# Retention layer and token/channel mixer on one core: decay on v instead of k in two batches, v of the first pair loaded first, tables made one by one

## The chip, the core and the metric

The kernel runs on one core of a Trainium2 chip. The metric is the device time of one execution in microseconds (us); the time given is the median of several executions. The engines are named as the profile names them: PE (matrix products; PEld is its weight load), DVE (vector engine), ACT (scalar engine), POOL (which here issues nearly all loads) and SP (which issues the first load, the transposes made by DMA, and most stores).

## The reference

For batch b (4), head h (8), 768 tokens and 64 dimensions a head, with a decay per head:

```
gamma = 1 - 2 ** (-5 - h);  scale = 1 / 8
state = gamma * state + outer(k[t], v[t])          # per token t
y[t]  = scale * q[t] @ state
x = y with heads side by side: [4, 768, 512]
h = relu(x^T @ w_tok1) @ w_tok2;   u = x + h^T     # mixing over tokens, 768 -> 256 -> 768
out = u + relu(u @ w_ch1) @ w_ch2                  # mixing over channels, 512 -> 1536 -> 512
```

## The kernel before, in words

Two heads form a pair; a batch has four pairs. In the text k00 is the k of batch 0, pair 0, and so on. `front(b, p)` handles a pair in six chunks of 128 tokens:

- Three loads bring k, q and v of the pair from fp32 in memory to fp16 in the core (line 284, and line 278 for the q of batches 0 and 1). Only k00 is loaded as fp32, by SP, into a buffer named `us` (set `HARD`, line 141).
- `decayed` (lines 322 for ACT, 324 for DVE) multiplies k by a decay per token, one instruction for each of the two heads; the result goes to a buffer of tag `k16`, of which there are three.
- `turn` transposes k and q. In batches 0 and 1 PE does it: k with six products of 128 by 128 (line 348), q with twelve that write 64 rows each, a head at a time (line 346). k is copied out of the bank by DVE or ACT (line 361). q is multiplied on the way out by a table `gq` (line 356), made by ACT from an exponential, 384 wide for each pair (line 222). In later batches most turns go through DMA transposes on SP.
- Products of k and v give the states of the chunks (line 377, ten small products); DVE accumulates them with decay (lines 387, 389); ACT or DVE spreads them into `r` (lines 398, 401).
- Scores are products of the turned k and q (line 417), masked by DVE (line 427); masked scores times v (line 438) and `r` times q (line 447) give y in a bank.
- Then come the token mixer, products with `wt1` (line 467), a relu (lines 476, 478), products with `wt2` (line 487), copies to u and X (lines 493, 503), and the turn of u (line 533, copied out at line 540, or by DMA).

`back(b)` is the channel mixer. In batches 0 and 1 `widen` multiplies u with `wc1` (line 571; 96 products of 128x384 a batch), with a relu on ACT (line 587). In batches 2 and 3 `widen7` does it with seven products in the place of eight (line 644), with sums on DVE and a relu of two tiles at once on DVE (line 690). `narrow7` multiplies by `wc2` (lines 785 and 795), keeps partial results (line 775) and adds them into X (line 802), which is stored (line 832).

The order of all this work, on every engine, the choice of engine where there are two, and the bank of each result are in one table, `PLAN` (line 40), read by `placed` (line 72). A `+` in it is followed by a number of products of zeros on PE that nobody reads (line 906, called fillers here). The costs written at each operation are those with which such a table was planned; they don't act when the kernel runs. Each engine's queue is in order.

Of the kernel before, what the change touches and what calls it, by code (L numbers as in the profile page):

```python
# [21 lines left out]
class Op:  # L22
# [18 lines left out]
    "04050b000f010d0c0g03020e1h11i00907+e1n4061j51o1p1l10a2r01k11R01m+32v50i2w0h1q1r1s2s11S11u26+91v411x0j2t31T01w1"  # L41
    "U01V51z08+31A01W1y0l1X10k1Y2452260m1t01B1Z1D42u0+125651E31027+32x22820293203360n2y0p2z212A+23531C0340222B0q362"
    "C2F511F02a60r2302I2D0+22d32b2e0o2J2E251G12H1H2N51I02G2K22L3f712M02c11J1K01L01M2f12O3i3j1N12g73711O00s2P12h1P43"
    "8393a3H02i00z3b1Q03c2j0u2m2k03I2l03D12Q42n03n12R3e072S03E13h2p62T0t2W0x3F73d02U00y3g3k02q12o12V03l3o3G12X04f60"
    "v3m04g3p02Z33q43012Y03r0A3s14b03Q65273Rah33t3U3w4c0ae63S3T3u03z43x04d73B3A13J53C1af4e0agai4J13y03v13K4K13LaO4a"
    "R7aSaPaj3Man60E3NaQ3Y2ao4L0ak4aT3OaC53P10waDalapaEaU73V63WaV3Z4M1aW4P04h10B3X1400aI74iam0DaL54QaJ414424RaX34S0"
    "CaMaK4304T4U4j4kaYaZ441d451aF4aG47az7aN1baA460aw5191eaBat65h1axauaH4lbf4ay1fbg4mav5i00H1a1c4o10530I4804N6aq7ar"
    "4pbhbi4bjas4sb334904Obk4q5j14rb44W26045k14n0b07b654Y4t1b10Gb54V0bo504ub2bl6bp4Z4v0bmb74w34xbc7bn4z0151gbu64a4X"
    "4y0bvb84A164B0544b9555bd0F5Q0ba51252be4F4Cbs7bq1817bb5300Kbr4D0bKbt05704G0bO55604H00L4E05R0bxbwbLby158bz65n3bM"
    "5W15o5900PbP0bA0M5X5l0bB5a5T05p5YbT5U05ZbNbD5b06r05dbC0bU05m60bGbX5q5rbE61bH5V5e0ca65sc65f00S5Sc75u1043bY06s0c"  # L50
    "b1cc75yc2bV35vcd6o0c35x6p00JcfbQ55t05w5C05z4bWc8cg00O0N5A7u10R6t5D620bRbZc95B0c05c0cj5F7c15E0ck14I5G631523bS65"
    "645H0co5I5L5J06667ch55K1cp6870Q69ci6u26b45M06a06c5g5O36e16v6d16q6wclbF6f6x5N06y5P06g06zcT3cs6cmct6W1cU6kcu6B02"
    "51cV6E0Wc50cE66A1cF6D6X0d23d3cG6h7v0cN5cO6Fcv6cw7x10Td4db2cx6CcP6J16Z1cQ3bI0cR6G0cH5cScIdc6K6i16Hcecn6l16j0726"
    "c41dd7017A76Y6m0cy2cK3czcJ8A17y07Bd547CcL0V7D6I173cAd8571cr0dw2dxd60X7EcM7FcZ7d7dyd96L074cW3d00Yd17z6M2cX7w756"
    "N76da7G0dh4cB777cCdq6dr6O08B0781de5cYcDbJ0di820dk2dldjdf6Pdsdn7dCdt3dm0UdodpdudgdDdz4dA8318CdFdvdG2796735dEdBd"
    "H1dN46Q06n6S7c6T0dL6R17ddO7a6V7b6U0e23dM0dY850dRdP7e6dQ08D0dS7H01758E07fdU7g08617h47ie0847K0Ze97e307j07L7J7k11"
    "47P57Q7l7IeadVdTed877M07N7m113dZeee18827O08G17n8H7R0898F8a7q7o07r08b7S77T8c7p08I8J8de7dI67U08K7Y7s08LdJe80ek12"
    "el7Vem7W0eb8f41267Z0818i80011ec0eo77t8g7X0ep18jev58M0e44et8h8N0126e5enew8Re6egeh8Pez8k4ef8n68e0eu08QeA9b08l8oe"
    "x8m08Oeq38q18p08rey0eC9G08S0ercq18s09808T9H18teK39c0eG8u0eD8weY78V1eM5eL8x08WeBdKeHeZ8v08y0991eIeNeJes10eOf29M"
    "49e69I9Nf028U09f8Y58X08Zf1ePf3eR9gf5eQ2900eS9194f69O9h9ieW9PeT9j9Qfc9dff5eUf46920eXfgfa950fh3fj9k1fb9R9J1f7ft4"  # L60
    "fkfdf8fv79aej1960eVfu930fmfif9fwfnfl2fx9l0136frfyfA9K0fK7fBfLfo9ofsfpfHfz3fF9pfqg06fCfY5fZfO9n9mfDfPfIfM2g2fGg"
    "1fNg39q19r9s09t0fRfEfe9ug59v1g46eE1gcg6fSeF0fQ3g7fJ9w29L9xgafWfTg8fU9y09zgb9Cg9gj69S0fX8zfVgdh17gegB979A09D09B"
    "0gCgD9E0gF4gf9T51309XgggM29UgG09WgKgk0gogH5gL09VgNgp1gEa11a2gIgO9Y39ZgQh20a00gP1a30gTa45a5a60gJghhn0gRgXgsgUa7"
    "aagt09FgYh0a81ei0gq4gl2giab0gZgrgmac1h35gxguh4gSa90gyhjdW1h6h82hB5h70hogvgnh9hagwadhb0hChkhchlhp1hD3hdhrhFhqhm"
    "hshfhEhghuhGh5hvhIht6hH4hwhJhzhehNi61hxhOhPgW1hS7hyi7hi1ic5hAiahU6hThKhVi80ibhWhXidiD2i9iehLhZiiiB0ifhMi0ighQi"
    "ki4in4iCgA0hY3iFihip5ioiEi1iqiriH6hRiGi2iPijisi5iIiJiuit1iviW7hh0i3imiKiziwiLiX0iAiNilixji3gz1iQiOiMiyiRiSjE2i"
    "UiTiY6jejgjk5j1iZjj0j31j20jp4j5jlgV1iVj4j7jF0dX1j0jfjnj60jmjhjo0jajG5j8jqjtj9jbjrjAjs0jBjCjDjujvjd0jJjL1jMjc0j"
    "HjwjK0jxjNjIjO0jPjy1jz1jQjW1jRjSjV0jTjUjY0jX1"
# [27 lines left out]
def kernel(  # L96
# [44 lines left out]
    HARD = {(0, 0, "k")}  # L141
# [22 lines left out]
    def one(eng, cost, emit):  # L164
        return [(eng, cost[0], cost[1], emit)]
# [127 lines left out]
    def front(b, p):  # L293
# [22 lines left out]
        def decayed(tag, src, dep, g, hard):  # L316
            dst, got = Slot(tag), []
            for j in range(2):
# [7 lines left out]
                got.append(op(either(emit, ACT=(506, 610), DVE=(335, 420) if hard else (232, 312)),  # L326
# [3 lines left out]
        K, kl = decayed("k16", KF, kd, gk, (b, p, "k") in HARD)  # L330

        def turn(src, dst, dep, mode):
# [31 lines left out]
        if TURN[b, p, "q"] == "w":  # L364
            qt = turn(QF, QT, [qd], "w")
        else:
            Q, ql = decayed("q16", QF, qd, gy, False)
            qt = turn(Q, QT, ql, "x")
# [570 lines left out]
```

## Time and profile before

| what | value |
|---|---|
| time, median of three runs | 187.66 us (187.24 to 189.37) |
| the profiled execution's own time | 188.25 us |
| its span in the trace | 186.5 us |
| PE busy | 178.7 us, 96% |
| DVE busy | 164.9 us, 88% |
| ACT busy | 122.6 us, 66% |
| POOL busy | 53.4 us, 29% |

The profiled execution took 1.75 us more than its span, and 0.59 us more than the median. Engines work side by side; a wait costs time where nothing else fills it. A busy PE isn't PE at its peak: the rows count a product from its start to the end of its result, so products that overlap fill the row though they may not follow each other at the full rate. Where a text speaks of an instruction's row, its columns are start, length, engine, line, operation, result <- operands with shapes, count, and in brackets the idle time before it and what ended it.

### The profile page before, as it was taken

Reading aid. Unit: us, or ns where it says so; the run is one execution under the profiler, and the core shown is the slowest. Engines: PE = TensorE matmul, PEld = TensorE weight load, DVE = VectorE, ACT = ScalarE, POOL = GpSimd, SP = SyncE. Lnnn points to the kernel's source line nnn. Section 1 sums busy time; section 2 is a strip of 40 time slices with the busy share of each in tenths; the row PEclk is TensorE's granted clock in tenths of the full one; section 3 lists DMA queues with packets and bytes.
Section 4 is the critical chain, followed back from the end, with each engine's and each line's share of the span. In section 5 each row is a group of like instructions: output and inputs, shape, how many; then the busy total and the mean of one; then the engine's idle time right before and its main releaser. Section 6 shows DMA issues by size and latency. Waiting matters only on the chain.

```text
span 186.5 us, 5228 instructions
## 1 busy us (share of the span) xinstructions
PE 178.7 (96%) x2083; PEld 135.6 (73%) x2083; DVE 164.9 (88%) x433; ACT 122.6 (66%) x284; POOL 53.4 (29%) x65
## 2 busy tenths in 40 slices
PE   7987999999999999999999999999999999999991
PEld 3554788676678988866668988875688986667880
DVE  3798999868999998989259999999999999799992
ACT  3668588857879775677885586999793425773220
POOL 8996775455422008902000750000000000000000
PEclk9999999999999999999999999999999999999999
DMA  8999999999999979999993999880533040511045
GB/s 117 163 159 196 179 175 191 179 193 205 178 162 150 137 78 131 181 182 194 158 218 65 114 148 134 143 189 22 88 98 102 37 118 10 218 62 54 4 158 182
DMA packets 94377, 25.51 MB, mean 137 GB/s; under 512 B 84368, under 2 KB 91536, under 8 KB 94352
## 3 DMA queue, kind: packets, MB, share of 16 engines
q0 software_dynamic: 67456, 13.18, 90.6%
q1 hardware_dynamic: 25168, 9.11, 26.6%
q10 hardware_dynamic: 1728, 2.88, 4.5%
q8 instruction: 16, 0.26, 0.6%
q14 instruction: 9, 0.07, 0.1%
HBM read 26.74 MB, written 6.29 MB: 177 GB/s over the span
## 4 chain that ended last, share of the span: by engine, by line
PE 82%; DMA 7%; DVE 6%; POOL 1%; issue 1%; ACT 1%; DVEq 0%; POOLq 0%
PE bank L571 17%; PE bank L644 15%; PE bank L785 15%; PE bank L795 11%; DMA q<-in_q_dram 7%; PE bank L487 6%; PE bank L467 5%; PE bank L417 3%; DVE X L802 3%; PE bank L438 3%; PE bank L447 2%; PE bank L346 1%; PE bank L377 1%; PE bank L533 1%; DVE hs L749 1%; DVE qT L356 1%
## 5 line engine op out<-in xcount | busy, mean ns | idle before, releaser
L571 PE MATMUL bank<-uT,wc 128*128 128x384 f16 x192 | 35.6, 326 | 0.2 <-DVE uT L540 0.2
L427 DVE TENSOR_TENSOR am<-bank,mask 128x384 f16<-128x384 f32 x64 | 32.8, 548 | 1.0 <-PE bank L417 0.9
L284 POOL DMA_DIRECT2D v<-in_v_dram x16 | 16.7, 1043 | 42.8 <-PE bank L447 22.1
L587 ACT ACTIVATE h<-bank 128x384 f16<-128x384 f32 x48 | 22.0, 494 | 8.4 <-PE bank L571 8.0
L571 PEld LDWEIGHTS <-wc 128*128 128x128 f16 x192 | 17.4, 98 | 9.7 <-DVE uT L540 0.2
L785 PEld LDWEIGHTS <-hs 128*128 128x128 f16 x216 | 20.4, 98 | 3.5 <-DVE hs L749 0.5
L775 ACT COPY us<-bank 128x256 f32<-128x256 f32 x29 | 10.6, 378 | 18.8 <-PE bank L785 18.2
L661 DVE TENSOR_TENSOR h<-bank,us 128x384 f16<-128x384 f32 x36 | 18.7, 550 | 1.7 <-PE bank L644 0.9
L785 PE MATMUL bank<-wsum,hs 128*128 128x256 f16 x144 | 19.5, 273 | 0.0
L656 ACT COPY us<-bank 128x384 f32<-128x384 f32 x36 | 16.4, 489 | 4.6 <-PE bank L644 3.7
L802 DVE TENSOR_TENSOR X<-X,bank 128x256 f32<-128x256 f32 x48 | 19.0, 412 | 0.1
L389 DVE SCALAR_TENSOR_TENSOR U<-U,gs,bank 128x64 f32<-128x64 f32 x64 | 16.5, 277 | 1.1
L284 POOL DMA_DIRECT2D k<-in_k_dram x15 | 15.4, 1035 | 6.6 <-ACT u L493 2.4
L493 ACT CAST u<-bank 128x384 f16<-128x384 f32 x27 | 12.5, 483 | 5.6 <-PE bank L487 5.3
L453 ACT CAST x<-bank 128x384 f16<-128x384 f32 x25 | 11.6, 489 | 6.3 <-PE bank L447 6.3
L795 PEld LDWEIGHTS <-h 128*128 128x128 f16 x144 | 13.7, 98 | 1.8 <-DVE am L427 0.2
L644 PE MATMUL bank<-hs,wsum 128*128 128x384 f16 x72 | 14.8, 326 | 0.0
L467 PE MATMUL bank<-x,wt 128*128 128x128 f16 x192 | 14.5, 219 | 0.1
L749 DVE TENSOR_TENSOR hs<-h 128x768 f16<-128x768 f16 x20 | 10.9, 551 | 3.7 <-ACT h L587 3.7
L487 PE MATMUL bank<-h,wt 128*128 128x128 f16 x192 | 14.2, 219 | 0.0
L802 DVE TENSOR_TENSOR X<-X,us 128x256 f32<-128x256 f32 (+1 forms) x25 | 13.0, 534 | 0.6 <-ACT x L453 0.5
L487 PEld LDWEIGHTS <-wt 128*128 128x128 f16 x192 | 12.1, 98 | 1.5
(86 smaller groups left out, 361.2 us busy)
## 6 DMA issues: line engine op xcount, KB each, us to landing
v<-in_v_dram POOLq DMA_DIRECT2D x16, 192.0 KB, 9.2
q<-in_q_dram POOLq DMA_DIRECT2D x16, 192.0 KB, 8.6
out_dram<-X SPq DMA_DIRECT2D x12, 256.0 KB, 2.4
k<-in_k_dram POOLq DMA_DIRECT2D x15, 192.0 KB, 8.5
wc<-in_moe_w_ch_dram POOLq DMA_DIRECT2D x5, 512.0 KB, 13.4
out_dram<-X ACTq DMA_DIRECT2D x10, 256.0 KB, 2.4
wt<-in_moe_w_tok_dram POOLq DMA_DIRECT2D x2, 384.0 KB, 8.9
wc<-in_moe_w_ch_dram POOLq DMA_DIRECT2D x2, 256.0 KB, 10.1
```

The lines of the kernel that those rows point to most:

```text
L284: (nc.sync if hard else nc.gpsimd).dma_start(out=s.tile, in_=src.rearrange("h (c p) d -> p h c d", p=P))
L389: nc.vector.scalar_tensor_tensor(out=u[:, c], in0=u[:, c - 1], scalar=gs[:, p:p + 1], in1=st, op0=ALU.mult, op1=ALU.add)
L427: nc.vector.tensor_tensor(am, SC[g].tile[:, :m * P].rearrange("p (i t) -> p i t", t=P), mask.to_broadcast([P, m, P]), ALU.mult)
L467: nc.tensor.matmul(acc[:, jt * P:(jt + 1) * P], wt1[:, i, jt * P:(jt + 1) * P], X16.tile[:, i], start=(i + jt == 0), stop=(i == NC - 1), s ...
L487: nc.tensor.matmul(Y[hf].tile[:, i * P:(i + 1) * P], wt2[:, jt, t], H1.tile[:, jt], start=False, stop=(jt == NJ - 1), skip_group_check=True)
L571: nc.tensor.matmul(acc[:, :SH], wc1[:, ct, ft * P:(ft + 1) * P], UT.tile[:, ct, sh * SH:(sh + 1) * SH], start=(ct == 0), stop=(ct == NP - 1))
L587: nc.scalar.activation(H2.tile[:, ft], A.tile[:, :SH], AF.Relu)
L644: nc.tensor.matmul(acc[:, :SH], left(ct), r[:, ct], start=first and ct == 0, stop=ct == 1, skip_group_check=True)
L661: nc.vector.tensor_tensor(into(hf)[:, ft], bank.tile[:, :SH], kept(j), ALU.add)
L785: nc.tensor.matmul(acc_[:, lo], l[:, j], r[:, j], start=first and j == 0, stop=j == K2 - 1, skip_group_check=True)
L795: nc.tensor.matmul(acc_[:, lo], l[:, j], r[:, j], start=first and j == 0, stop=j == K2 - 1, skip_group_check=True)
L802: (nc.vector if e == "DVE" else nc.gpsimd).tensor_tensor(dst(), dst(), b_(), ALU.add)
```

## The change

In batches 0 and 1 (`ON_V`) the decay multiplies v instead of k, still in a buffer of tag `k16`; k goes to its turn and to the state products as it was loaded. The two forms are equal, since only the product of k and v, or of the scores and v, is used. As k is then laid out a head at a time, its turn on PE takes twelve products with 64 rows instead of six with 128. The first pair's v is the load that comes as fp32 through SP, and its k comes through POOL. The table `gq` becomes four operations, of which each pair waits for its own. The turn of u of batch 0's last pair uses two banks instead of one, and the relu over two tiles in `widen7` may go to ACT (six of eighteen do). `PLAN` is another table: fillers go from 37 to 30.

```diff
-    "04050b000f010d0c0g03020e1h11i00907+e1n4061j51o1p1l10a2r01k11R01m+32v50i2w0h1q1r1s2s11S11u26+91v411x0j2t31T01w1"
+    "000501020i0304071k10e0g1l10a+h1q11r+31o31s1m0060d0h0l1Y51n01t0b0j0f0c1p1u09081v1Z+41W01X01x460m1y321A+327501U0"
...
-    HARD = {(0, 0, "k")}
+    HARD = {(0, 0, "v")}
+    ON_V = (0, 1)
...
-    def emit():
-        for p in range(NP):
+    gq_ops = []
+    for p in range(NP):
+        def emit(p=p):
             nc.scalar.activation(gq[:, p], SINCE.tile.rearrange("p a b -> p (a b)")[:, :SH], AF.Exp, bias=lnsc, scale=lnh[:, p:p + 1])
-    gq_op = prep("ACT", 2490, emit, [since_op, lnh_op, lgs_op], (-20, 0, -1, 1), uses=[SINCE])
+        gq_ops.append(prep("ACT", 622, emit, [since_op, lnh_op, lgs_op], (-20, 0, -1, 1), uses=[SINCE]))
...
-        K, kl = decayed("k16", KF, kd, gk, (b, p, "k") in HARD)
+        on_v = b in ON_V
+        if on_v:
+            K, kl = KF, [kd]
+            V, vl = decayed("k16", V, vl, gk, (b, p, "v") in HARD)
+        else:
+            K, kl = decayed("k16", KF, kd, gk, False)
+            vl = [vl]
...
+            halves = mode == "w" or src is KF
...
-                    if mode == "w":
+                    if halves:
                         for j in range(2):
                             nc.tensor.transpose(tp[rows_of(j), c * P:(c + 1) * P], src.tile[:, j, c], ident16)
...
-                return op(one("DVE", (870, 950), emit), [t, gq_op], [dst], [T])
+                return op(one("DVE", (870, 950), emit), [t, gq_ops[p]], [dst], [T])
...
-                        def emit(hf=hf, ft=ft):
+                        def emit(e, hf=hf, ft=ft):
                             h = H[hf].tile[:, ft:ft + 2]
-                            nc.vector.tensor_scalar(h, h, 0.0, None, ALU.max)
+                            if e == "ACT":
+                                nc.scalar.activation(h, h, AF.Relu)
+                            else:
+                                nc.vector.tensor_scalar(h, h, 0.0, None, ALU.max)
```

How instructions move is shown at three places. The first is POOL's queue, from the q of batch 0's last pair on (before) and from the token weights on (now). Ahead of this piece nine loads were issued before: v00, q00, q02, k02, k01, q01, v01, k03, v02. Now eight are: k00, q00, q01, k01, v01, k02, q02, v02. `wt` is `wt1` and `wt2`, `wc_80` is `wc1`. Before:

```order
L278 DMA q<-in_q_dram 128x2x384
L260 DMA wt_78<-in_moe_w_tok_dram 128x6x256
L260 DMA wt_79<-in_moe_w_tok_dram 128x2x768
L284 DMA v<-in_v_dram 128x12x64
L278 DMA q<-in_q_dram 128x2x384
L284 DMA k<-in_k_dram 128x12x64
L278 DMA q<-in_q_dram 128x2x384
L260 DMA wc_80<-in_moe_w_ch_dram 128x4x256
L284 DMA k<-in_k_dram 128x12x64 x2
L284 DMA v<-in_v_dram 128x12x64
```

Now, from the same place in the program:

```order
L262 DMA wt_78<-in_moe_w_tok_dram 128x6x256
L262 DMA wt_79<-in_moe_w_tok_dram 128x2x768
L280 DMA q<-in_q_dram 128x2x384
L286 DMA k<-in_k_dram 128x12x64
L286 DMA v<-in_v_dram 128x12x64 x2
L286 DMA k<-in_k_dram 128x12x64 x2
L286 DMA v<-in_v_dram 128x12x64
L280 DMA q<-in_q_dram 128x2x384 x2
L262 DMA wc_80<-in_moe_w_ch_dram 128x4x256 x2
```

Before, these are q03, wt1, wt2, v03, q10, k10, q11, the first part of `wc1`, k11, k12 and v10. Now they are wt1, wt2, q03, k03, v03, v10, k10, k11, v11, q11, q10 and two parts of `wc1`. The first thirteen loads that POOL issues are those of batch 0 and the token weights in both kernels (with k00 in the place of v00); q10 moves from the fourteenth place to the nineteenth, and the first part of `wc1` from the seventeenth to the twentieth.

The second place is ACT's queue at the start, behind the small tables. `k_...` is a decay's result (of tag `k16`), `gq` the table for q, `kT` the turned k. Before:

```order
L322 ACTIVATE k_121<-us,gk 128x6x64
L222 ACTIVATE gq<-us,lnsc,lnh 128x384 x4
L322 ACTIVATE k_188<-k,gk 128x6x64
L322 ACTIVATE k_192<-k,gk 128x6x64
L361 COPY kT<-bank_259 128x768
L398 ACTIVATE r_329<-U,gp 128x5x64 x2
```

Now:

```order
L224 ACTIVATE gq<-us,lnsc,lnh 128x384 x2
L376 COPY kT<-bank_175 128x768
L224 ACTIVATE gq<-us,lnsc,lnh 128x384 x2
L376 COPY kT<-bank_231 128x768
L324 ACTIVATE k_277<-v,gk 128x6x64 x2
L413 ACTIVATE r_351<-U,gp 128x5x64 x2
```

ACT no longer takes half of the first decay (both halves are on DVE), the turned k no longer waits behind a decay, and the decays on ACT read v.

The third place is PE at the end of the turn of k10. `bank_681` before and `bank_691` now take the turned k; `bank_708` takes the states, and `k_605` is the decayed v10, in a buffer of tag `k16`. Before, the turn was followed by masked scores times v:

```order
L348 MATMUL bank_681<-ident_75,k_624 128x128
L438 LDWEIGHTS am
L438 MATMUL bank_697<-v,am 128x64
```

Now:

```order
L361 LDWEIGHTS k
L361 MATMUL bank_691<-ident_75,k 64x128
L392 LDWEIGHTS k
L392 MATMUL bank_708<-k_605,k 64x64
```

The turn now stands directly ahead of the pair's state products, which are of the same 64-row kind; runs of 64-row products on PE (turns of k and q, and states) are 18 before and 21 now, 8 and 9 of them behind the first product with `wc1`.

More of the change, by code (lines that the diff above doesn't have):

```diff
@@ L69 @@
+    "0jC0jFjMgY1j3jO5jbjB1jN0jGjcjdjQjR0jf1jPjSjejTjUjWjVjXk01k11jg0jY0"
 )
@@ L325, in emit @@
                                                                                ALU.mult)
-                got.append(op(either(emit, ACT=(506, 610), DVE=(335, 420) if hard else (232, 312)),
+                got.append(op(either(emit, ACT=(506, 610), DVE=(800, 900) if hard else (232, 312)),
                               [dep, g_op], [] if got else [dst], ([dst] if got else []) + [src],
@@ L349, in emit @@
                                             ident16)
-            t = op(one("PE", (340, 500), emit), dep + [ident_op], [T], [src], tiled="high" if mode == "w" else "")
+            t = op(one("PE", (340, 500), emit), dep + [ident_op], [T], [src], tiled="high" if halves else "")
             if mode == "w":
@@ L367, in front @@
             Q, ql = decayed("q16", QF, qd, gy, False)
-            qt = turn(Q, QT, ql, "x")
+            qt = turn(Q, QT, ql, TURN[b, p, "q"])
         two_before = y_done.get(b * NP + p - 2)
@@ L438, in emit @@
                         nc.tensor.matmul(y[:, i * P + j * D:i * P + (j + 1) * D], AM[2 * hf + j].tile[:, i],
-                                         V.tile[:, j, hf * HC + i], start=(i + j == 0), stop=False, skip_group_check=True)
-            y = op(one("PE", (175, 335), emit), [am_ops[2 * hf + j] for j in range(2)] + [vl], [Y[hf]],
+                                         v_of(hf * HC + i, j), start=(i + j == 0), stop=False, skip_group_check=True)
+            y = op(one("PE", (175, 335), emit), [am_ops[2 * hf + j] for j in range(2)] + vl, [Y[hf]],
                    [V] + [AM[2 * hf + j] for j in range(2)])
@@ L687, in block @@
                     for hf, ft in ((0, i - 1), (1, K2 + i - 1), (0, K2 + i - 1)):
-                        def emit(hf=hf, ft=ft):
+                        def emit(e, hf=hf, ft=ft):
                             h = H[hf].tile[:, ft:ft + 2]
-                            nc.vector.tensor_scalar(h, h, 0.0, None, ALU.max)
-                        rel[hf][ft] = rel[hf][ft + 1] = op(one("DVE", (265, 350), emit), [rel[hf][ft], rel[hf][ft + 1]],
+                            if e == "ACT":
+                                nc.scalar.activation(h, h, AF.Relu)
+                            else:
+                                nc.vector.tensor_scalar(h, h, 0.0, None, ALU.max)
+                        rel[hf][ft] = rel[hf][ft + 1] = op(either(emit, DVE=(265, 350), ACT=act(2 * SH, sbuf=1)), [rel[hf][ft], rel[hf][ft + 1]],
                                                            [], [H[hf]])
```

76 lines of the change are left out of this document (40 added, 36 removed).

## Prediction

> **What bounds the kernel now.** I read the page first, then PE's share by stretches of time, then the chain of work that ended last, then POOL's queue. On the page PE is busy almost throughout:
>
> ```profile
> PE 178.7 (96%) x2083; PEld 135.6 (73%) x2083; DVE 164.9 (88%) x433; ACT 122.6 (66%) x284; POOL 53.4 (29%) x65
> ...
> PE   7987999999999999999999999999999999999991
> ```
>
> The windows (busy PE, PEld, DVE, ACT, POOL; granted clock, DMA share, GB/s) show that it is full from 35 us on, and not at the start:
>
> ```profile
> 15.00:20.00 5.00, 3.86 (x65) 2.37 (x63) 4.16 (x14) 3.75 (x8) 2.86 (x5) 1.00 1.43 198
> 35.00:40.00 5.00, 5.00 (x66) 3.46 (x64) 3.46 (x10) 3.20 (x9) 2.80 (x3) 1.00 1.73 187
> 170.00:175.00 5.00, 5.00 (x48) 4.26 (x46) 4.97 (x13) 1.26 (x4) 0.00 (x0) 1.00 0.01 3
> ```
>
> The chain (start, length, what) tells the same in order of time. Two loads of q make up much of the first 18 us; from 20.8 us it goes mostly through PE, still with pieces of other engines, and from 34.31 us products follow each other without a gap that matters.
>
> ```profile
> 3.28 4.72 DMA q<-in_q_dram
> 8.05 0.55 PE bank L346 x12
> ...
> 10.32 7.71 DMA q<-in_q_dram
> 18.07 0.55 PE bank L346 x12
> ...
> 20.77 0.83 PE bank L467 x12
> ...
> 31.43 0.60 PE bank L571 x3
> 32.04 0.67 PE bank L487 x12
> ...
> 33.90 0.37 DVE uT L540
> 34.27 0.04 issue
> 34.31 1.79 PE bank L571 x10
> ```
>
> So the end is set by two things: when PE begins to run without gaps (34.31 us), and how much PE work is left then. At the end PE's last products stand close behind each other, and the adds and stores behind them are the same kind and number in the new order, so I cost the tail at nothing:
>
> ```profile
> 181.66 0.82 PE L785 MATMUL bank<-wc,hs 128*128 128x256 f16 x6
> ```
>
> **The start: loads.** POOL's rows show how fast data comes. A row's wait ends when the load eight places before it has landed:
>
> ```profile
> 23.85 0.74 POOL L260 DMA_DIRECT2D wc<-in_moe_w_ch_dram  x1 [0.27 <-DMA q<-in_q_dram]
> ...
> 32.49 0.74 POOL L260 DMA_DIRECT2D wc<-in_moe_w_ch_dram  x1 [0.52 <-DMA wc<-in_moe_w_ch_dram]
> ...
> 40.09 0.70 POOL L278 DMA_DIRECT2D q<-in_q_dram  x1 [1.24 <-DMA wc<-in_moe_w_ch_dram]
> ...
> 50.28 1.01 POOL L284 DMA_DIRECT2D k<-in_k_dram  x1 [1.59 <-DVE am L427]
> ```
>
> The first is the 22nd load and waits for the 14th, q10, which so landed at 23.8; the second is the 29th and waits for the 21st, a part of `wc1`, landed at 32.45; the third is the 33rd, for the 25th (the last of `wc1`, 40.05); the last is the 38th, for the 30th (the last of `wc2`), where the row names a DVE operation that I take to be long done. From the 14th to the 21st a load costs (32.45 - 23.8) / 7 = 1.24 us, and the 13th landed near 22.6. The first thirteen are the same loads in both kernels but for k00 in the place of v00, so v03, now the 13th, lands at 22.6, and q10, now the 19th behind v10, k10, k11, v11 and q11, at 22.6 + 6 x 1.24 = 30.0; four of these six are k or v, and I take 30.5.
>
> What PE must do ahead of its first product with `wc1` is, last in its order: turn q10, then the products with `wt2` of pair 3. Rows for the turns, with what follows them, so that the time from start to start can be read:
>
> ```profile
> 36.76 0.50 PE L348 MATMUL bank<-ident,k 128*128 128x128 f16 x6
> 37.09 0.49 PE L571 MATMUL bank<-uT,wc 128*128 128x384 f16 x2
> ...
> 47.14 0.53 PE L346 MATMUL bank<-ident,q 128*64 128x128 f16 x12
> 47.60 0.66 PE L571 MATMUL bank<-uT,wc 128*128 128x384 f16 x3
> ...
> 60.33 0.51 PE L377 MATMUL bank<-v,k 128*64 128x64 f16 x20
> 60.67 0.51 PE L346 MATMUL bank<-ident,q 128*64 128x128 f16 x12
> 61.11 0.83 PE L785 MATMUL bank<-wsum,hs 128*128 128x256 f16 x6
> ```
>
> A turn with twelve 64-row products takes 0.46 us, one with six takes 0.33. So the first product with `wc1` can start at 30.5 + 0.46 + 0.67 = 31.6, by the loads.
>
> **The start: ACT.** The decay of v03 (landed 22.6) heads a queue on ACT that ends in the relu of pair 3, for which the `wt2` products wait. Rows:
>
> ```profile
> L503 ACT COPY X<-bank 128x384 f32<-128x384 f32 x27 | 13.0, 496 | 0.3 <-DVE u L493 0.2
> L493 ACT CAST u<-bank 128x384 f16<-128x384 f32 x27 | 12.5, 483 | 5.6 <-PE bank L487 5.3
> L453 ACT CAST x<-bank 128x384 f16<-128x384 f32 x25 | 11.6, 489 | 6.3 <-PE bank L447 6.3
> L322 ACT ACTIVATE k<-k,gk 128x384 f16<-128x384 f16 x17 | 10.2, 621 | 3.4 <-DMA k<-in_k_dram 3.4
> L690 DVE TENSOR_SCALAR h<-h 128x768 f16<-128x768 f16 x18 | 6.0, 353 | 0.1
> L476 ACT ACTIVATE h<-bank 128x256 f16<-128x256 f32 x14 | 5.4, 388 | 5.2 <-PE bank L467 5.2
> L361 ACT COPY kT<-bank 128x768 f16<-128x768 f16 x4 | 3.2, 795 | 1.2 <-PE bank L348 1.2
> ...
> L540 ACT COPY uT<-bank 128x768 f16<-128x768 f16 x2 | 1.6, 798 | 0.4 <-PE bank L533 0.4
> L324 DVE TENSOR_SCALAR k<-us,gk 128x384 f16<-128x384 f32 x1 | 0.7, 670 | 1.9 <-DMA us<-in_k_dram 1.9
> ```
>
> In the new order these are three decays (3 x 0.62), three casts to u (3 x 0.48), two copies to X (2 x 0.50), two casts to x (2 x 0.49), a relu and the last one (2 x 0.39), one turned u (0.80) and one turned k (0.80): 7.7 us. Ahead of the decay stands a cast of pair 2, which I put at 23.4 us, so the last relu ends at 31.1, where q10's turn ends too (30.5 + 0.46 = 31.0). The two limits meet; I put the first product with `wc1` at 31.7. Behind it the new order has twelve such products with the turn of u's last pair between them, with a wait for copies as before (33.90 us in the chain), which ACT now makes, from two banks. In the chain three such products take 0.60 and ten 1.79, so each further one (1.79 - 0.60) / 7 = 0.17 us; twelve and the turn (0.33) are 2.4 us, so PE runs full from about 34.1 us.
>
> **What is done by then.** At 34.31 before: six `wc1` products, pair 0's scores of batch 1, its states, and both its first turns of k. At 34.1 now, by the order: twelve `wc1` products, states of two pairs of batch 1, no scores. The difference is 6 products more (6 x 0.17 = 1.0), one run of states more (20 products take 0.34 to the next row, so 0.17), scores less (0.44, half-way between 0.33 and the 0.55 of the turns' rows, the nearest), so 0.75 us of work ahead, and 0.2 us earlier: 1.0 us gained.
>
> **The turns of k.** Eight of them now have the dearer form, at up to 0.46 - 0.33 = 0.13 us each. Six lie before 34.1 us and are in the walk above. But the extra isn't the products: in the last rows above a turn of q behind state products costs 0.44 and the states ahead 0.34 for twenty, so the extra belongs to the change from one form to the other, and the order now puts such runs together: 21 of them in place of 18, and 9 in place of 8 behind the first `wc1` product. I take one such extra behind 34.1 us, 0.13 us; the bounds are 0 and 2 x 0.13. The Trainium skill (TensorEngine Tiling (Array Packing), Key Properties) says that a change of the tiling mode drains the PE. That speaks against this change, since every turn of k in batches 0 and 1 now asks for another mode; if each of the eight drained by itself it would cost 8 x 0.13 = 1.0 us, by runs it is 3 x 0.13 = 0.4 us. The trace agrees with the drain.
>
> **The other edits.** v00 as fp32 is decayed by DVE alone, 2 x 0.67 instead of 0.67 beside ACT's half: 0.7 us later, but the q that the first scores need lands only at 8.0 us in the chain, so nothing. The tables one by one let the turned k pass on ACT in the first 10 us, also under that load: nothing. Six relus leave DVE (6 x 0.35 = 2.1 us) for ACT; the nearest row of that width on ACT is the turned k at 0.80, so 4.8 us on an engine that is idle a third of the time, in a stretch where PE's row is full. That is 0, with a bound of +0.8 us for one that is waited for. Fewer fillers: nothing, since PE stands idle where they stood.
>
> **Sum.** -1.0 + 0.13 = -0.9 us. Against the profiled execution, 188.25 - 0.9 = 187.4 us; it stood 0.59 above the median, so against the median 187.66 - 0.9 = 186.8 us.
>
> **The rivals.** First, faster: the start pays out whole. q10 at the 30.0 of the plain mean, with ACT's casts at a shorter distance than their rows, brings the full stretch 0.7 us forward, and no later change of form costs anything: -1.0 - 0.7 - 0.2 = about 185.7 us. For it: ACT's rows overlap, so that 7.7 us is an upper sum. Against: a wait per link that my sum leaves out.
>
> Second, no gain: ACT's queue of pair 3 starts later, since its first link, the cast of pair 2, hangs on q03 and k03, now 11th and 12th loads. Each us there moves the full stretch by one; at 1 us late the gain is gone, 187.7 us.
>
> Third, slower: the weights. Those of the channel mixer now stand behind all of batch 1's q and k. The last part of `wc2` is now the 33rd load, three more than before, so 50.25 + 3 x 1.24 = 54.0 us. By the order PE has some 24 us of work (94 products of 0.17 are 16, the rest smaller ones) between the first `wc1` product and the first with `wc2`: 31.7 + 0.4 + 24 = 56.1. The margin is 2.1 us. From there each us of lateness in the loads is a us of PE: if they slip 5 us (a gap in POOL's queue, whose copies of `gp` now stand behind five loads instead of nine), the time is 186.8 + 2.9 = 189.7 us. For it: DMA is busy all through that stretch. Against: POOL's requests run eight loads ahead.
>
> **How the numbers follow.** My forecast has 0.50, the faster rival 0.20, no gain 0.17, the weights 0.13. About 1% (1.9 us) is what a measurement of this kernel can tell from no change. Faster by over 1% means under 185.8: the faster rival's larger part and the lower edge of mine, 0.22. Slower means over 189.5: nearly all of the weights' case and a little of the second, 0.15. The rest is 0.63. The range from 185.2 to 188.8 leaves out the far ends of the first and third rivals, about 2 in 10.
>
> **What would show it.** In the changed kernel's chain the first `wc1` product stands at 31 to 32.5 us with twelve of them done by 34.5; the first product with `wt1`, at 20.77 before, comes 2 to 4 us earlier, as pairs 0 to 2 are loaded ahead of q03. The turn of k ahead of states takes 0.33 to 0.46. From 35 us PE's row is full as before. Wrong would be: a PE wait for a DMA of `wc` between 40 and 56 us; a PE wait for DVE or ACT in the later batches, where the order is new too and where I assume that it is as dense as the old one; or a first `wc1` product after 33 us.

## The result, and the profile after

| what | before | after |
|---|---|---|
| time, median | 187.67 us (187.24 to 189.37, 4 runs) | 189.88 us (189.56 to 190.22, 4 runs) |
| ratio of the times | | 1.0103, 95% interval 1.0069 to 1.0138 |
| the profiled execution's own time | 188.25 us | 189.82 us |
| its span | 186.5 us | 188.0 us |

The change made the kernel 1% slower, where 0.9 us less was forecast. The time lies 1.1 us above the range. The ratio on record is worked out from the fast runs of both kernels; the quotient of the two medians is 1.0118.

The page of the changed kernel shows PE nearly full again, with one thing that the page before does not have, a weak place in the middle (slices 22 and 23 of 40, at 99 to 108 us, read 7 and 8):

```profile
PE 178.9 (95%) x2124; PEld 135.1 (72%) x2124; DVE 167.0 (89%) x432; ACT 125.1 (67%) x283; POOL 53.4 (28%) x65
...
PE   7898989999999999999997899999999999999993
```

The windows around it, of the changed kernel and then of the kernel before (busy PE, PEld, DVE, ACT, POOL; granted clock, DMA share, GB/s):

```profile
95.00:100.00 5.00, 5.00 (x74) 4.43 (x73) 4.94 (x11) 3.60 (x9) 5.00 (x6) 1.00 1.48 140
100.00:105.00 5.00, 3.85 (x52) 3.26 (x50) 3.91 (x10) 1.66 (x4) 0.67 (x1) 1.00 2.15 110
105.00:110.00 5.00, 4.41 (x69) 3.73 (x68) 4.33 (x17) 4.70 (x13) 2.03 (x2) 1.00 2.06 159
```

```profile
100.00:105.00 5.00, 5.00 (x78) 4.55 (x77) 4.91 (x13) 3.09 (x8) 1.40 (x2) 1.00 0.89 116
105.00:110.00 5.00, 5.00 (x88) 4.63 (x85) 4.82 (x17) 3.08 (x9) 4.65 (x5) 1.00 2.13 132
```

PE loses 1.15 us in the one stretch and 0.59 in the other, and ACT does little in the first (1.66 us). The clock stays at 1.00. I call this the hole. It is 1.7 us of PE's row, more than the 1.5 us by which the spans differ. What stands in it is read from four timelines of the changed kernel (start, length, engine, line, what, count, idle time before and its releaser): PE's, ACT's, POOL's and SP's.

```profile
102.50 0.51 PE L432 MATMUL bank<-qT,kT 64*128 64x128 f16 x12 [1.15 <-DMA qT<-q]
106.18 0.33 PE L462 MATMUL bank<-r,qT 128*128 128x128 f16 x3 [0.25 <-ACT r L413]
107.57 0.81 PE L814 MATMUL bank<-wc,h 128*128 128x256 f16 x6 [0.35 <-ACT X L518]
```

```profile
104.10 1.12 ACT L324 ACTIVATE k<-k,gk 128x384 f16<-128x384 f16 x2 [3.26 <-DMA k<-in_k_dram]
```

```profile
94.63 1.01 POOL L286 DMA_DIRECT2D v<-in_v_dram  x1 [10.35 <-PE bank L462]
95.62 3.03 POOL L286 DMA_DIRECT2D k<-in_k_dram  x3
```

```profile
94.75 2.94 SPq L350 DMA_TRANSPOSE qT<-q  x2
```

There are two late transfers. First, the load of k31 (batch 3, pair 1) stands on POOL's queue behind that of v31, which waits 10.35 us for one of the four v buffers; k31 is issued at 95.6 us, ACT's decay waits for it until 104.10, and r, u and X, which PE then waits for, stand behind the decay on ACT. Secondly, the q of batch 2's pair 3 (q23) is turned by DMA, issued by SP at 94.75 us, and PE waits for it at 102.50. Without the wait PE would have wanted it at 101.35, 6.6 us after the issue. In the kernel before the same places look like this (PE, then SP):

```profile
97.40 0.51 PE L417 MATMUL bank<-qT,kT 64*128 64x128 f16 x12
101.73 0.51 PE L417 MATMUL bank<-qT,kT 64*128 64x128 f16 x12
```

```profile
85.19 3.13 SPq L336 DMA_TRANSPOSE qT<-q  x2
88.43 6.41 SPq L336 DMA_TRANSPOSE kT<-k  x2
```

Its q turns (of pairs 2 and 3) are issued at 85.19 and some 1.6 us later, 12 and 15 us ahead of the products that use them.

The start is the place that the forecast was about. The chain of the changed kernel:

```profile
27.40 0.82 DVE r L416
28.59 0.68 DVE k L326
29.27 0.47 DVE X L518
29.79 0.84 PE bank L482 x12
30.64 0.79 PE bank L361 x24
31.43 0.78 PE bank L502 x12
32.20 0.49 PE bank L587 x3
...
34.49 0.33 PE bank L432 x7
```

The first `wc1` product (L587) starts at 32.0 in PE's row, and PE has no gap from about 34.5 on, much as forecast (31.7 and 34.1). But ahead of it the chain goes through DVE, not through ACT. The end is no later than the rest: PE's last products begin at 183.97 us (181.66 before), 2.3 us later, and the adds and stores behind them are 0.8 us shorter.

### The profile page after: what moved, and what is told of

Read it like the earlier page. It is cut to its first block, busy times and chain, and to the rows that moved or that the text cites. A ratio compares the mean times of both kernels' runs of the same rounds, so it can differ in the third digit from the quotient of the medians.

```text
span 188.0 us, 5320 instructions
## 1 busy us (share of the span) xinstructions
PE 178.9 (95%) x2124; PEld 135.1 (72%) x2124; DVE 167.0 (89%) x432; ACT 125.1 (67%) x283; POOL 53.4 (28%) x65
## 4 chain that ended last, share of the span: by engine, by line
PE 70%; DVE 15%; DMA 8%; ACT 2%; POOL 2%; issue 1%; DVEq 0%; POOLq 0%; ACTq 0%
PE bank L587 16%; PE bank L804 13%; PE bank L660 12%; PE bank L814 9%; DMA k<-in_k_dram 8%; PE bank L502 5%; PE bank L482 4%; DVE am L442 3%; PE bank L432 3%; DVE hs L768 3%; DVE h L677 2%; PE bank L453 2%; DVE X L821 2%; PE bank L361 2%; PE bank L462 2%; DVE U L404 2%
## 5 line engine op out<-in xcount | busy, mean ns | idle before, releaser
L587 PE MATMUL bank<-uT,wc 128*128 128x384 f16 x192 | 35.5, 326 | 0.0
L442 DVE TENSOR_TENSOR am<-bank,mask 128x384 f16<-128x384 f32 x64 | 32.1, 547 | 2.7 <-PE bank L432 2.6
L286 POOL DMA_DIRECT2D v<-in_v_dram x15 | 15.5, 1038 | 46.1 <-PE bank L453 29.1
L587 PEld LDWEIGHTS <-wc 128*128 128x128 f16 x192 | 17.4, 98 | 9.5 <-issue 0.2
L404 DVE SCALAR_TENSOR_TENSOR U<-U,gs,bank 128x64 f32<-128x64 f32 x64 | 17.2, 275 | 1.0
L286 POOL DMA_DIRECT2D k<-in_k_dram x16 | 16.6, 1046 | 3.4 <-PE bank L587 1.7
L502 PE MATMUL bank<-h,wt 128*128 128x128 f16 x192 | 15.0, 219 | 0.0
L502 PEld LDWEIGHTS <-wt 128*128 128x128 f16 x192 | 12.2, 98 | 2.1
L468 ACT CAST x<-bank 128x384 f16<-128x384 f32 x27 | 12.5, 487 | 1.7 <-PE bank L462 1.5
L482 PEld LDWEIGHTS <-wt 128*128 128x128 f16 x192 | 12.0, 98 | 1.4 <-DVE X L518 0.3
## 6 DMA issues: line engine op xcount, KB each, us to landing
v<-in_v_dram POOLq DMA_DIRECT2D x15, 192.0 KB, 10.4
```

Source lines behind the costliest of these rows:

```text
L286: (nc.sync if hard else nc.gpsimd).dma_start(out=s.tile, in_=src.rearrange("h (c p) d -> p h c d", p=P))
L404: nc.vector.scalar_tensor_tensor(out=u[:, c], in0=u[:, c - 1], scalar=gs[:, p:p + 1], in1=st, op0=ALU.mult, op1=ALU.add)
L442: nc.vector.tensor_tensor(am, SC[g].tile[:, :m * P].rearrange("p (i t) -> p i t", t=P), mask.to_broadcast([P, m, P]), ALU.mult)
L482: nc.tensor.matmul(acc[:, jt * P:(jt + 1) * P], wt1[:, i, jt * P:(jt + 1) * P], X16.tile[:, i], start=(i + jt == 0), stop=(i == NC - 1), s ...
L502: nc.tensor.matmul(Y[hf].tile[:, i * P:(i + 1) * P], wt2[:, jt, t], H1.tile[:, jt], start=False, stop=(jt == NJ - 1), skip_group_check=True)
L587: nc.tensor.matmul(acc[:, :SH], wc1[:, ct, ft * P:(ft + 1) * P], UT.tile[:, ct, sh * SH:(sh + 1) * SH], start=(ct == 0), stop=(ct == NP - 1))
```

## The experiments

The kernels are told in the order of the questions, not of the runs. All times stand against the kernel before on the same chip (medians 187.8 to 188.2 us); a ratio is the one on record with its 95% interval, which can differ from the quotient of the two medians by up to 0.2%. Where only the order is changed, the diff shows the order of the loads on POOL's queue from v30 on, or that of the turns on SP's.

**The k load behind v31.** One load is moved:

```diff
-v30 q31 q22 k23 k30 q23 q30 v31 k31 k33 k32 q33 v32 v33 q32
+v30 q31 q22 k23 k30 q23 q30 k31 v31 k33 k32 q33 v32 v33 q32
```

> As the run before, but only one k (batch 3, pair 1) is issued ahead of that v; the k of pairs 3 and 2 stay behind it and are still issued near 95.6 us, beside the DMA turn of q that PE waits 1.15 us for at 101.4 us. Theory A with ACT's wait as its whole: the same gain as with three, 1.8 to 2.6 us. Rival C (the q turn lands late because of the loads beside it): the wait for q stays, the gain is 0.8 to 1.5 us.

189.01 us, ratio 1.0052 (1.0025 to 1.0078): 0.9 us of the loss comes back. PE's row shows what is left:

```profile
102.41 0.51 PE L432 MATMUL bank<-qT,kT 64*128 64x128 f16 x12 [0.51 <-ACT k L324]
```

k31 is now issued at 84.4 us, 11 us sooner, and ACT's wait is gone. The last wait stands at the same product as before and is put down to ACT, but the turn of q23, issued at 95.41, took 6.9 us to land, so at 102.3: it is the turn that was late.

**Three k loads ahead of v31.**

```diff
-... q30 v31 k31 k33 k32 q33 v32 v33 q32
+... q30 k31 k33 k32 v31 q33 v32 v33 q32
```

> The changed kernel with one load moved in POOL's queue: v of batch 3, pair 1 is issued behind the three k of that batch (pairs 1, 3, 2) that stood behind it; nothing else is changed. Theory A (the loss is POOL's queue: that v waits 10 us for a free buffer until 94.6 us, the k behind it land late, ACT stands at the decay of one of them until 104 us, and PE goes short from 100 to 110 us): the PE windows from 100 to 110 us fill up again, ACT's wait of 3.3 us is gone, and the time falls by 1.8 to 2.6 us, to 187.3 to 188.1 us, at or a little under the kernel before. Rival B (the loss is spread: the dearer turns of k and the relus on ACT): under 0.5 us, 189.4 us or more. Rival C (the q turn's DMA and its loads collide, whoever is first): about half, 1.1 us.

191.95 us, ratio 1.0197 (1.0159 to 1.0236): 2 us worse than the change itself, a miss. k32 waited for a buffer in its turn, until 89.9 us, and v31 behind it came at 96.6; the turns of 88 to 98 us had the loads beside them and PE waited twice for qT. Its profiled execution took 195.1 us, 3 us more than the median, and the granted clock fell to 0.50 behind the second of these waits (108.5 to 111.7 us), so the prices of the waits are not read from it.

**Other places for the loads.** Five more orders ask whether the rest of the hole is the crowd of loads beside the turns.

```diff
 e5
-v21 v30 q31 q22 k23 k30 q23 q30 v31 k31 k33 k32 q33 v32 v33 q32
+v21 q31 q22 k23 k30 q23 q30 k31 k33 v30 v31 k32 q33 v32 v33 q32
 e6
+v21 q31 q22 k23 k30 q23 q30 v30 k31 k33 v31 k32 q33 v32 v33 q32
 e9
+v21 v30 q31 q22 k23 k30 q23 q30 v31 k31 v32 k33 k32 q33 v33 q32
 e10
+v21 v30 q31 q22 k23 k30 q23 q30 k31 v31 v32 k33 k32 q33 v33 q32
 e11
+v21 v30 q31 q22 k23 k30 q23 q30 k31 v31 v32 v33 k33 k32 q33 q32
```

> The changed kernel with its loads in another order on POOL's queue: q31, q22, k23, k30, q23, q30, k31 and k33 stand right behind v21, ahead of v30 and v31, which wait for a free v buffer at 77 us and 94.6 us. Nothing else moves. Theory Q (the hole at 100 to 110 us comes from loads that stand behind a v load that waits): all eight can go from 57 us on, k31's decay on ACT no longer waits (3.3 us now), nor the q turn at 94.75 us (1.15 us on TensorE): 187.9 to 188.4 us, better than the 189.0 us with k31 alone ahead. Theory T (loads and DMA turns share the DMA engines, so that a load hurts wherever it lies beside a turn): the eight now lie beside the turns of 61 to 71 us and the five outputs at 72 us, which come late: 189.5 to 191.5 us, with waits for qT or kT at 65 to 80 us.

> The changed kernel with q31, q22, k23, k30, q23 and q30 right behind v21, ahead of v30, and k31 and k33 right behind v30, ahead of v31. Theory Q: as in the run with eight, since v30's buffer is free at 77 us and k31 is wanted only at 100 us: 187.9 to 188.4 us. Theory T: six loads beside the turns of 61 to 71 us, two at 78 to 88 us where there are none: 189 to 190.5 us. If it lies at 188.4 to 189.0 us, the queue was it only in part: then k31's wait is gone and the q turn of 95 us, beside k32, q33 and v32, still waits.

> The changed kernel with v32 ahead of k33, k32 and q33 on POOL's queue, right behind v31 and k31. v32 waits for its buffer until some 98 to 100 us, so that the three come 2 to 4 us later and the q turns issued at 94.75 and 96.3 us share the DMA engines with two loads instead of five. k31 stays behind v31. Theory T (crowded turns make the hole): the turns land some 2 us sooner, TensorE's 1.15 us for qT goes, k31 lands at 102 instead of 104 us: 188.3 to 189.0 us. Theory Q (k31's place behind v31 makes it): only k31's wait counts, 189.4 to 190.0 us.

> The changed kernel with both: k31 ahead of v31, and v32 ahead of k33, k32 and q33. If queue and crowding each hold a part, the hole of 100 to 110 us closes: 187.2 to 188.3 us, below the 189.0 us of k31 alone ahead by 0.7 to 1.5 us. If the crowding by those three is worth nothing, it stays at 189.0 us.

> As the run with both, but v33 too ahead of k33, k32 and q33, so that these three wait with it until 107 us and no turn of 88 to 103 us has more than v31 and v32 beside it. Theory T: the q turns of 95 us land in 5 us or less and TensorE's wait at 102 us is gone; what is new is that k32 and k33 land at 116 us, where ACT wants them at 114 to 115 us: 187.5 to 189.0 us. If the time is above 189.5 us, those two are late and the hole has moved to 112 to 120 us.

Measured: e5 189.90 us (1.0106, 1.0074 to 1.0137), e6 190.06 (1.0104, 1.0068 to 1.0139), e9 190.21 (1.0127, 1.0090 to 1.0163), e10 188.95 (1.0044, 1.0017 to 1.0071), e11 196.75 (1.0461, 1.0422 to 1.0501). e10 is e2 again; the others are no better than the change. In e5, e6 and e10 k31 is in time and ACT's wait is gone, and still PE waits for q23's turn, 1.7, 1.4 and 1.8 us. In e11 the three loads were put off to 108 us and later, and a k that ACT needs came too late; the summary of waits, and then the windows:

```profile
PE bank L814 <- ACT X L518: 5.6, 1, 5.6
PE bank L432 <- DMA qT<-q: 1.1, 1, 1.1
```

```profile
108.00:113.00 5.00, 0.40 (x4) 0.21 (x3) 1.24 (x6) 0.00 (x0) 4.33 (x5) 0.83 1.67 107
```

Yet in e11 only v31 and v32 lay beside q23's turn. The view of the DMA issues (count, median us from issue to landing) gives that turn of 95.66 us as the first row; the second row is the turn of k at 92 to 93 us in the changed kernel, when nothing was loaded:

```profile
qT<-q SPq DMA_TRANSPOSE x1, 6.9
```

```profile
kT<-k SPq DMA_TRANSPOSE x1, 2.8
```

So a turn alone lands 2.8 us after its issue, and one load or two beside it are enough for 7 us. Thinning the crowd gains next to nothing as long as v31 is loaded at 95 us; a lead of 6.6 us is too short in all of these orders.

**The same bytes in fewer packets.** The loads of k33, k32, q33 and v32 in longer rows, which puts the tokens of these tiles in another order, so that pairs 2 and 3 of batch 3 are computed from tokens in a wrong order:

```diff
+                if (b, p, what) in ((3, 3, "k"), (3, 2, "k"), (3, 3, "q"), (3, 2, "v")):
+                    nc.gpsimd.dma_start(out=s.tile.rearrange("p h c d -> p h (c d)"),
+                                        in_=src.rearrange("h (p c) d -> p h (c d)", c=NC))
```

> The changed kernel with the four loads k33, k32, q33 and v32 (issued at 96.6 to 100 us) read in rows of 768 bytes where they are read in rows of 128 bytes: the same bytes, a sixth of the packets, the tokens of these four tiles in another order, so that the heads of the last two pairs of batch 3 are computed from tokens in a wrong order. The order of all instructions stays. Theory T: the q turn issued at 94.75 us and k31's load no longer share the DMA engines with four slow loads: TensorE's 1.15 us for qT goes and k31 lands some 3 us sooner: 188.0 to 188.6 us. Theory Q: k31 is still issued only at 95.6 us behind v31 and lands 8 us later, ACT's 3.3 us stay for the larger part: 189.3 to 189.9 us.

191.37 us, ratio 1.0170 (1.0123 to 1.0217): slower, against both theories. DMA issues from 94.3 to 95.9 us, of the changed kernel and of this one (the k is k31, the turn is q23's):

```profile
k<-in_k_dram POOLq DMA_DIRECT2D x1, 192.0 KB, 8.4
...
qT<-q SPq DMA_TRANSPOSE x1, 7.6
```

```profile
k<-in_k_dram POOLq DMA_DIRECT2D x1, 192.0 KB, 10.4
...
qT<-q SPq DMA_TRANSPOSE x1, 7.4
```

Beside fewer but longer packets q23's turn lands no sooner to speak of, and what got worse is k31's load: it takes 2 us longer, and PE's wait for ACT's r grows from 0.25 to 1.83 us. The turn behind q23's takes 10.8 us, against 9.1 in the changed kernel. These are single executions; in e3, with the loads in short rows, k31 took 9.6 us and the two turns 7.9 and 9.7. The Trainium skill (DMA: Bandwidth & Descriptors, Queues, rings and completion order) says that each DMA engine goes round the queues packet by packet; by that a neighbour with longer packets would take more of the engine. The second turn agrees with this, q23's does not, and no run here shows the order of packets itself.

**The crowd in the kernel before.** Two loads are put beside the turns of 85 to 95 us there.

```diff
 before
-k31 k30 q30 v31 q31 v30 v33 q33 k32 q32 k33 v32
+k31 k30 q30 v31 q31 v30 q33 k32 v33 q32 k33 v32
```

> The kernel before with two loads, q33 and k32, taken from behind v33 (105 us) to behind v30 (85.8 us), beside the q turns of 85.2 us and the k turns of 88.4 us. All else stays. Theory T: the turns, which already take 6.4 us for two there, land 2 to 4 us later and TensorE or DVE waits for them at 90 to 102 us: 188.3 to 190 us. Rival (the order before issues its turns early enough to hide any crowding): 187.4 to 188.2 us.

188.13 us, ratio 1.0005 (0.9987 to 1.0022): nothing lost; the rival held. DMA issues from 84 to 90 us, of the kernel before and of this one:

```profile
qT<-q SPq DMA_TRANSPOSE x2, 9.2
kT<-k SPq DMA_TRANSPOSE x1, 7.9
```

```profile
qT<-q SPq DMA_TRANSPOSE x2, 11.1
kT<-k SPq DMA_TRANSPOSE x1, 13.4
```

The turns do land later, by 1.9 us (the median of the two of q) and 5.5 us (that of k), and PE waits for none of them. The crowding costs nothing there: the q turns are issued 12 and 15 us ahead of their products, and they take 11.1 us.

**The turn's place.** That left the lead of q23's turn. It changes places with the turn of q31, which PE wants only at 111 us: load, two decays and turn, in the changed kernel (e13), with k31 ahead as well (e14), and with k31 ahead and the loads early (e15).

```diff
 SP's turns of q, e13, e14 and e15
-q22 q31 q23 q30
+q22 q23 q31 q30
 POOL's loads
-v21 v30 q31 q22 k23 k30 q23 q30 v31 k31 k33 k32 q33 v32 v33 q32
 e13
+v21 v30 q23 q22 k23 k30 q31 q30 v31 k31 k33 k32 q33 v32 v33 q32
 e14
+v21 v30 q23 q22 k23 k30 q31 q30 k31 v31 k33 k32 q33 v32 v33 q32
 e15
+v21 q23 q22 k23 k30 q31 q30 v30 k31 v31 k33 k32 q33 v32 v33 q32
```

> The changed kernel with the q of batch 2's pair 3 (wanted by TensorE at 101.4 us, loaded at 82 us, turned at 94.75 to 96.3 us) and the q of batch 3's pair 1 (wanted at 111 us, loaded at 78 us, turned at 90.7 us) in each other's places: load, the two decays and the turn. The counts on each engine and queue stay. Theory L (the hole is a turn issued 5 to 7 us ahead of its use, where the kernel before has 12 to 16 us): TensorE's 1.15 us for qT at 102.5 us goes; k31 still lands at 104 us and holds ACT, so that 0.3 to 1.0 us is gained of 189.9: 188.9 to 189.6 us. Rival (the turn's place is worth nothing as long as k31 is late): 189.7 to 190.2 us.

> The same exchange, and k31 ahead of v31 on POOL's queue. Theory L with theory Q (a late turn and a late k load, each with a part of the hole): neither wait is left at 100 to 107 us, the whole 2.0 us hole closes: 187.2 to 188.2 us, 0.8 to 1.8 us below the 189.0 us with k31 alone ahead. Rival (a third wait stands behind the two): 188.6 to 189.2 us.

> The same exchange, with the loads of q23, q22, k23, k30, q31 and q30 right behind v21, ahead of v30, and k31 right behind v30, ahead of v31. The earlier run with the loads early kept 1.3 us of the hole, at the q turn. Theory L: with the turn 4 us earlier this goes too, 187.2 to 188.4 us. Theory T (early loads crowd the turns at 61 to 75 us instead): 188.8 to 190 us.

e13 took 190.45 us (1.0123, 1.0086 to 1.0160; a little above both of its expectations), e14 187.33 us (0.9982, 0.9959 to 1.0004), e15 187.58 us (0.9983, 0.9959 to 1.0007). The turn alone gains nothing; with the k load the whole hole closes, 2.3 us by the ratios (1.0103 - 0.9982 = 1.2% of 188). The windows of e14, and its SP and PE rows:

```profile
100.00:105.00 5.00, 5.00 (x87) 4.28 (x85) 5.00 (x13) 3.83 (x11) 0.00 (x0) 1.00 1.98 117
105.00:110.00 5.00, 5.00 (x69) 4.33 (x65) 4.89 (x18) 4.39 (x10) 2.03 (x2) 1.00 1.87 153
```

```profile
91.13 1.24 SPq L350 DMA_TRANSPOSE qT<-q  x1
```

```profile
100.84 0.51 PE L432 MATMUL bank<-qT,kT 64*128 64x128 f16 x12
```

PE is full; q23's turn is issued 9.7 us ahead of its product, which no longer waits. PE's order is the same in e14 as in the changed kernel, so their products can be compared one by one: e14 is 0.4 us ahead at 100 us, from the start, and 2.6 us ahead at 110, and it stays so to the last products, at 181.42 and 183.97 us. In these two executions the two transfers cost 2.1 us, all of it between 100 and 110 us. In e13 the product with q23 doesn't wait either (101.18 us, 1.3 us sooner than in the changed kernel), but ACT still stands until 104.13 for k31, and PE then loses in one piece what it lost in two:

```profile
106.20 0.33 PE L462 MATMUL bank<-r,qT 128*128 128x128 f16 x3 [1.60 <-ACT r L413]
...
107.59 0.84 PE L814 MATMUL bank<-wc,h 128*128 128x256 f16 x6 [0.35 <-ACT X L518]
...
108.44 1.49 PE L804 MATMUL bank<-wc,hs 128*128 128x256 f16 x6
```

**The relus on ACT.** Six two-tile relus are done on ACT in the changed kernel. Three runs move them: back to DVE in the changed kernel (e3), to ACT in the kernel before (e8), back to DVE in e14's order (e16). The code of e8:

```diff
-                            nc.vector.tensor_scalar(h, h, 0.0, None, ALU.max)
+                            if on_act:
+                                nc.scalar.activation(h, h, AF.Relu)
+                            else:
+                                nc.vector.tensor_scalar(h, h, 0.0, None, ALU.max)
```

In e3 and e16 the same six entries of `PLAN` name DVE.

> The changed kernel with its six relus over two tiles back on DVE, at the same places of the order. Prediction's step (moving them costs nothing, bound 0.8 us): within 0.4 us of 189.9. Rival B: if ACT's longer relus hold PE, 0.5 to 0.8 us less. If DVE needed the relief, up to 2 us more.

> The kernel before with the six two-tile relus of the channel mixer (five in batch 2, one in batch 3) that the changed kernel has on ACT done on ACT as well. All else stays. Theory V (DVE binds the channel mixers in either order; the changed kernel lost 1.5 us when its six went back to DVE): 186.3 to 187.3 us. Rival (the relief is worth something only in the order that the changed kernel has, where DVE is late): 187.6 to 188.3 us.

> The version with the q of batch 2's pair 3 first and k31 ahead of v31 (187.3 us), with the six two-tile relus of the channel mixer back on DVE. If the six relieve DVE in the later batches by themselves, the 1.5 us that they cost in the changed kernel's order come back: 188.5 to 189.1 us. If most of that 1.5 us was the hole growing (a late DVE made the q decays and with them the q turn later), it is worth little here: 187.3 to 187.9 us.

e3 took 191.36 us (1.0175, 1.0143 to 1.0208), e16 188.49 us (1.0034, 1.0009 to 1.0059), e8 190.24 us (1.0122, 1.0082 to 1.0163). So on ACT the six save 1.0 us in e14's order, where there is no hole (1.0034 - 0.9982). In the changed kernel's own order it is 1.4 us (1.0175 - 1.0103), but there the hole differs too: PE waits 1.8 us for q23's turn in e3, against 1.15. In the old order they cost 2 us or a little more, against both of e8's expectations. One takes 868 ns on ACT and 351 on DVE, as the groups of the changed kernel show:

```profile
L707 ACT ACTIVATE h<-h 128x768 f16<-128x768 f16 x6 | 5.2, 868 | 0.7 <-DVE h L677 0.7
L709 DVE TENSOR_SCALAR h<-h 128x768 f16<-128x768 f16 x12 | 3.9, 351 | 0.1
```

In the old order the copies that PE waits for stand behind them on ACT; the summary of waits of e8 from 110 us on has this, where the kernel before has 0.6 us of the first and none of the second:

```profile
DVE h L661 <- ACT us L656: 3.0, 4, 1.1
...
PE bank L644 <- ACT us L656: 0.7, 2, 0.4
```

**The turns of k.** The kernel before with the turns of k in batches 0 and 1 as twelve products of 64 rows, the order untouched:

```diff
+                    elif b < 2:
+                        for j in range(2):
+                            nc.tensor.transpose(tp[rows_of(j), c * P:(c + 1) * P], src.tile[:, c, j], ident16)
```

> The kernel before with one part of the change: the turn of k in batches 0 and 1 uses twelve products with 64 rows (a head at a time) instead of six with 128, of the decayed k as before, in the old order, where the turns stand apart from other products of this form. Prediction's price: 0.13 us for each change of form that is not hidden by the start; four of the eight turns stand behind 33 us, so +0.5 us (0.3 to 0.7), 188.2 us. Rival (the products themselves are dearer, or weights of 64 columns load slower): 1 us or more. Rival: no measurable difference.

188.91 us, ratio 1.0067 (1.0042 to 1.0092): 1.1 to 1.3 us dearer, where 0.3 to 0.7 was expected. PE's rows, and then the row that stands ahead of the turn of 36.76 us in the kernel before:

```profile
36.49 0.33 PE L574 MATMUL bank<-uT,wc 128*128 128x384 f16 x1
36.74 0.53 PE L349 MATMUL bank<-ident,k 128*64 128x128 f16 x12
37.20 1.80 PE L574 MATMUL bank<-uT,wc 128*128 128x384 f16 x10
```

```profile
36.60 0.33 PE L571 MATMUL bank<-uT,wc 128*128 128x384 f16 x1
```

From start to start the turn takes 0.46 us, against 0.33 before. But the product ahead of it takes longer too: 0.25 us to the start of the turn (36.49 to 36.74), against 0.16 (36.60 to 36.76). So a turn that stands alone costs 0.13 + 0.09 = 0.22 us, one part at each edge. Four of the eight turns stand behind 27 us, and each shows both parts in PE's rows: 0.9 us. The other four lie at the start, where PE waits anyway; what they cost is not seen in the rows.

## Why the prediction was wrong

**The step that failed** is the one that I named as an assumption and gave no term: that the order in the later batches "is as dense as the old one". It isn't. It lets q23's turn begin 6.6 us ahead of its use and k31's load stand behind v31's wait, and these two cost 2.3 us. Each was hidden by the other, so that the turn alone gains nothing, the load alone 0.9 us, and both together 2.3 us. With both in time the changed kernel takes 187.33 us in the order that e14 has, inside the range, 0.5 us above the forecast, and not to be told from the kernel before (0.9959 to 1.0004); where its missing 0.5 us went was not taken apart. The rows of POOL's and SP's queues in the later batches, which the change rewrites too, have no place in the sum: it follows POOL's queue only to the last weights, at 54 us.

**The start.** The place was right, the size a little large. In the 14 profiled executions that share this start the first `wc1` product came at 30.9 to 32.2 us, half of them below 31.8; the forecast was 31.7. For the gain I count PE's products by their spacing in a run (0.163 us for 384 columns, 0.109 for 256, 0.056 for 128): the work left at 60 us is 0.5 to 0.8 us less than before in the mean of the 14, against three executions of the old start, and 0.3 to 0.6 us less in the changed kernel's own profiled execution (the smaller figure leaves out the products of 64 columns, the larger counts them as half of 128). That is an estimate, beside 1.0 in the sum. Of the two limits, ACT's queue came as forecast: its last relu ended at 31.05 us (forecast 31.1). The loads were not a limit: q10 landed at 29.2 us, 1.3 us sooner than forecast. In the chain it was DVE's work on scores and states from 24 to 30 us that stood last. How far that one engine alone sets it was not tried.

**The turns of k.** 0.13 us for a turn that stands alone was too small: it counted the edge behind the turn and left out the one ahead, and e4's rows give 0.22. The sum took one, so that is 0.1 us. In the changed kernel the last two turns of k stand in one run with two turns of q:

```profile
37.92 1.46 PE bank L361 x48
```

That is 0.37 us each, so a turn among others of its form has next to no extra, as the sum by runs had it. Standing alone in e4's order they cost 0.22 each in the rows and 1.1 to 1.3 us in all by the time. The Trainium skill's rule on the change of the tiling mode (TensorEngine Tiling (Array Packing), Key Properties) fits both.

**The relus** I had at 0 with a bound of +0.8. They are a gain of 1.0 us, a sign I had not given a bound for. With the relus on DVE (e16) PE's products fall 0.9 us behind those of e14 from 120 us on; 0.6 us there are waits of PE for DVE, against 0.2 in e14. ACT's 0.80 us for one was near the 0.87 measured.

**The rest.** Together: 0.6 us slower with both transfers in time and the relus on DVE (e16), 1.0 less for the relus, 2.3 more for the hole, 1.9 in all, which is the ratio of 1.0103. So without the relus the change would not have gained its 0.9 us even in a dense order; against the kernel before, e16 loses its lead from 140 us on, by the work left. DVE is nearly full there, but so it is before (19.4 and 19.5 of the 20 us from 130 to 150 us). What in the order there costs it was not taken apart.

**The rivals.** The weights of the channel mixer were in time: the first product with `wc2` came at 56.4 us (forecast 56.1) without a wait for them. ACT's late queue did not decide either. The slower case that came true was not among my rivals; it stood only in the last sentence, without a chance.

## What to carry to other kernels

When a new order of work is forecast, read for each DMA turn and each load the time between its issue and its use, over the whole kernel and not only around the change; what is written in the diff as a faster start can be paid for by a lead that has shrunk elsewhere. A lead below what the transfer takes in company (7 us here, against 2.8 alone) is a wait. If two late transfers feed the same stretch, taking away one shows little or nothing: take away both before you call either harmless.

## What the runs showed of the hardware

A DMA turn that takes 2.8 us alone took 6.9 us beside two loads of 192 KB (e11), and up to 13 us in a crowd (e12). Longer rows in the neighbours did not help: 7.4 us against 7.6 for q23's turn, and 10.4 against 8.4 for k31's load.

After a hole PE itself ran slower in some executions. In e13's profiled execution PE had done little from 104.6 to 106.2 us, and the six products at 108.44 took 1.49 us where 0.82 is usual; the windows of that stretch give the granted clock:

```profile
106.00:108.00 2.00, 1.45 (x33) 1.17 (x33) 1.08 (x6) 2.00 (x7) 0.46 (x1) 1.00 1.82 155
108.00:110.00 2.00, 2.00 (x14) 1.54 (x13) 0.92 (x5) 1.56 (x5) 1.57 (x2) 0.56 2.25 174
110.00:112.00 2.00, 2.00 (x16) 1.66 (x15) 1.33 (x5) 1.01 (x2) 0.00 (x0) 0.58 1.97 156
```

From 112 us it is 1.00 again. Four microseconds at 0.57 are another 1.7 us. In e11 the clock was 0.83 in the nearly empty window shown above and 0.50 in the next five microseconds, and in e1 it was 0.50 behind a wait of 2.4 us. In the changed kernel the shorter waits left it at 1.00. The Trainium skill (TensorE: Matmul & The Clock Gate, What's actually happening) puts the half clock behind an idle window of some 3.4 us; here 1.6 us without a product and 0.35 soon after were enough in one execution. The length of a wait does not decide it alone: e3 and e10 have a wait of 1.8 us each, e7 has two, of 1.5 and 1.8 us, and their clock stays at 1.00 from 98 to 113 us. What does decide it was not tested.

Nor is the hole shown to be the only cause of a lower clock. Of e13's six runs two have a mean clock of 0.988 and 0.991, the others 0.997 or more, but the kernel before, which has no hole, has a run of 189.41 us with 0.991 too, and no trace shows where in it the clock fell.
